# Three PSUM tiles in place of two and a remainder for the transposed q and k, and the threshold searches moved to other batches, in a top-32 attention followed by a squared-ReLU block

## The chip, the cores and the metric

The kernel runs on one core of a Trainium2 chip. The metric is the device time of one execution in microseconds (us); the median of three runs stands for a kernel. One further execution was recorded by the hardware profiler, and all rows shown come from it. The engines are TensorE (PE, with its weight loads shown apart as PEld), VectorE (DVE), ScalarE (ACT), GpSimd (POOL) and the DMA queue of SyncE (SP).

## The reference

Eight batches, eight heads, 576 positions, head size 64. Each row of scores keeps its 32 largest values, softmax is taken over these, and the result goes through two dense layers with a squared ReLU between them.

```python
scores = scale * np.matmul(q, k.transpose(0, 1, 3, 2))        # 8 x 8 x 576 x 576
kth = np.partition(scores, -32, axis=-1)[..., -32:-31]
scores = np.where(scores >= kth, scores, -1e9)
attn = np.exp(scores - scores.max(-1, keepdims=True)); attn /= attn.sum(-1, keepdims=True) + 1e-9
x = (attn @ v) with the heads of a row side by side           # 4608 x 512
out = np.maximum(x @ w_in, 0) ** 2 @ w_out                    # 512 -> 2048 -> 512
```

## The kernel before

Work on the attention is cut into *groups*: 128 query rows of the two heads of a *pair* (there are 4 pairs in a batch, 32 in all). A batch has 4 pairs by 4 full groups, and two further groups that collect the 64 rows left over of two pairs: 18 groups a batch, 144 in all.

For each pair, q and k are loaded by DMA into the tiles `rq` and `rk` (five blocks of 128 rows, the last one with 64, both heads side by side). PE transposes each block into PSUM and ACT copies the result into the tile `qk`, whose 1216 columns are q (576), the last 64 rows of k, k's 512 others, and the last 64 again. `first_pair` does this for pair 0 in its own way, `load_pair` for the 31 others. In `load_pair`, four blocks of q go into one PSUM tile `tq`, four of k into `tk`, and the two small blocks into `tx`; four ACT copies (L711 to L714) empty them. These tiles come from the pool `psum`, which has two banks of PSUM and also serves the output of the attention and of the dense layers.

For each group, `score` computes the scores on PE into three banks of PSUM, and ACT copies them to the tile `s` (L755). Then `top_k` finds the 32nd largest of each row: DVE folds the row into maxima (L905), POOL forms what is left over from the folds in integer arithmetic (L900, three instructions), and DVE takes eight maxima and strikes them out in turn (L939, L943, L934), until L946 gives the threshold `kth`. ACT makes a mask from it (L965), PE transposes scores and mask into PSUM, ACT takes the exponential (L1021), PE multiplies by v, and POOL divides by the row sums (L1096). The dense layers follow in chunks of rows: PE, ReLU on ACT (L1140), the square on POOL or ACT (L1152, L1155), PE, a copy (L1172) and a DMA to the output.

Four of the 144 groups get their threshold in another way, by `hunt`: ACT counts how many values of a row lie above a trial threshold (six rounds of two instructions at L776, each followed by a read of the accumulator), POOL moves the trial threshold by what was counted (L783, tiny instructions), and at the end one POOL multiplication (L812) and two DVE maxima (L814) read the 32nd value off the few that are left. A hunt is put into the order of groups a number of places ahead of the group that needs it. The dictionary `HUNT` names these groups as (batch, pair, block) and the number of places. A hunted group leaves out the chain of DVE instructions of `top_k`, and POOL's three. At the end the kernel looks whether every threshold is proven; if one isn't, a second, plain program runs all over again.

Nothing is ordered by hand. A planner (`Plan.schedule`) runs when the program is built: every operation has an engine, an assumed duration, and a priority in us; whenever an engine is free in the plan, the ready operation with the lowest priority value takes it. The order so found is fixed for each engine. The chip then runs each engine in this order, with semaphores for what one needs of another, so an instruction that has to wait holds up all behind it on its engine. `tg` is the due time of a group, 5.3 us (`PER`) after the one before; round j of a hunt is due at `tg + HO + HS * j`. The planner also sets short dummy matmuls where PE would be idle.

Of the kernel before, what the change touches and what calls it, by code (L numbers as in the profile page):

```python
# [13 lines left out]
P = 128  # L14
# [370 lines left out]
def bass_top_k_attn__then__act_relu_squared_kernel(  # L385
# [24 lines left out]
    def sb(name, shape, dt=FP32, n=None):  # L410
        if n is None:
            return nc.alloc_sbuf_tensor(name, shape, dt)
        return [nc.alloc_sbuf_tensor(f"{name}{i}", shape, dt) for i in range(n)]
# [31 lines left out]
    LATE = 2.3  # L445
    LAGL = 11.07
    LAGE = 2.5
    HN, HA, HP, HZ, HS, HD, HO = .3, .86, .68, 2.18, 5, 32, 22

    ident32 = sb("ident32", [P, P])  # L450
    ident_bf = sb("ident_bf", [P, P], BF16)
# [10 lines left out]
    c16 = sb("c16", [P, 2, NGRP + 8])  # L462
    c24 = sb("c24", [P, 2, NGRP + 8])
    rzall = sb("rzall", [P, NALL])
    HUNT = {(2, 2, 3): 12, (3, 2, 3): 12, (4, 2, 3): 12, (5, 2, 3): 11}
    NH = len(HUNT)
    NSTEP = 4
    GAIN = (.014, .008, .005, .003)
# [38 lines left out]
    def tile(nm):  # L507
        return Tile(pools[nm])

    def at(t):  # L510
        x = mem[t.pool.name][t.slot]
        if t.pool.name in ("hs", "hz"):
            c = 8 if t.pool.name == "hs" else 10
            return x[:, c:c + 2 * S].rearrange("p (i c) -> p i c", i=2)
        if t.pool.name in ("s", "u"):
            n_ = 2 * (S if t.pool.name == "s" else HALF + QUART)
            return x[:, t.phase:t.phase + n_].rearrange("p (i c) -> p i c", i=2)
        return x

    def bank(t, i=0):  # L520
        return ps32[:, BASE[t.pool.name] + t.slot + i, :]
# [9 lines left out]
    act, vec, gp, pe = nc.scalar, nc.vector, nc.gpsimd, nc.tensor  # L531
# [52 lines left out]
    def tr(o, i, ident, **kw):  # L584
        return pe.matmul(o, i, ident, is_transpose=True, skip_group_check=True, **kw)  # L585
# [3 lines left out]
    def build(full, weights, pl):  # L589
# [7 lines left out]
        def load_first(b, hp, rq, rq2, rk, base):  # L597

            def part(t, src, h, tb, n_):
                r0 = 128 * tb + (64 if h and src is k else 0)  # L600
                return at(t)[:, tb:tb + n_, h, :], src[b, 2 * hp + h, r0:r0 + 128 * n_, :].rearrange(
                    "(tb p) d -> p tb d", p=P)

            def rest(t, src, r0, d0):
                x = src[b, 2 * hp, r0:r0 + 64, :]
                return at(t)[0:64, 4, :, :], bass.AP(x.tensor, x.offset, [x.ap[0], [(S + d0) * D, 2], x.ap[1]])

            def start(queue, *parts):
                return lambda: [queue.dma_start(*x()) for x in parts]

            both = bass.AP(q.tensor, q[b, 2 * hp, 0:P, :].offset, [[D, P], [S * D, 2], [1, D]])
            pl.op("sp", .1, base - 82, start(nc.scalar, lambda: part(rk, k, 0, 0, 4),
                                             lambda: rest(rk, k, REST[0], REST[1] - REST[0])),
                  w=[rk], take=[rk], sem=slot_sem, ndma=2, via="act")
            pl.op("sp", 4.0, base - 81, start(nc.sync, lambda: part(rk, k, 1, 0, 4)), w=[rk], sem=lambda o: "first", ndma=1)
            pl.op("sp", 3.5, base - 80, start(nc.sync, lambda: (at(rq)[:, 0, :, :], both)), w=[rq], take=[rq],
                  sem=slot_sem, ndma=1)
            pl.op("sp", 3.5, base - 79, start(
                nc.sync, lambda: part(rq2, q, 0, 1, 3), lambda: part(rq2, q, 1, 1, 3), lambda: rest(rq2, q, 512, 0)),
                w=[rq2], take=[rq2], sem=slot_sem, ndma=3)  # L620
# [32 lines left out]
        def load_pair(b, hp, base):  # L653
            rq, rk, rv = tile("rq"), tile("rk"), tile("rv")


            def load(t, src, rest):
                def fn():
                    r = at(t)
                    res = []  # L660
                    for h in range(2):
                        r0 = 64 if h and rest != (512, 512) else 0
                        res.append(nc.sync.dma_start(r[:, 0:4, h, :], src[b, 2 * hp + h, r0:r0 + 512, :].rearrange(
                            "(tb p) d -> p tb d", p=P)))
                    x = src[b, 2 * hp, rest[0]:rest[0] + 64, :]
                    res.append(nc.sync.dma_start(r[0:64, 4, :, :], bass.AP(
                        x.tensor, x.offset, [x.ap[0], [(S + rest[1] - rest[0]) * D, 2], x.ap[1]])))
                    return res
                return fn

            def loadv():
                r = at(rv)
                res = [nc.sync.dma_start(r[:, 4 * h:4 * h + 4, :], v[b, 2 * hp + h, 64 * h:64 * h + 512, :].rearrange(
                    "(tb p) d -> p tb d", p=P)) for h in range(2)]

                for h in range(2):
                    res.append(nc.sync.dma_start(r[64 * h:64 * h + 64, 8 + h, :], v[b, 2 * hp + h, REST[h]:REST[h] + 64, :]))
                return res

            via = not full and not state["pairs"]  # L680
            state["pairs"] += 1
            if via:
                rq2 = tile("rq")
                load_first(b, hp, rq, rq2, rk, base)
            else:
                pl.op("sp", 2.3, base - 80, load(rq, q, (512, 512)), w=[rq], take=[rq], sem=slot_sem, ndma=3,
                      bw=BW * 1.9)
                pl.op("sp", 2.3, base - 79.9, load(rk, k, REST), w=[rk], take=[rk], sem=slot_sem, ndma=3, bw=BW * 1.9)
            pl.op("sp", 2.3, base - 70, loadv, w=[rv], take=[rv], sem=slot_sem, ndma=4, bw=BW * 1.9)
            qk, vb = tile("qk"), tile("vb")  # L690
            if via:
                return first_pair(rq, rq2, rk, rv, qk, vb, base)
            tq, tk, tx = Tile(psum), Tile(psum), Tile(psum)

            def t4(o, src):
                def fn():
                    for tb in range(4):
                        ins = tr(bank(o)[:, 128 * tb:128 * tb + 128], at(src)[:, tb, :, :].rearrange("p h d -> p (h d)"), ident32[:, :])
                    return ins
                return fn  # L700

            def t5():
                for i, s in enumerate((rq, rk)):
                    ins = tr(bank(tx)[:, 64 * i:64 * i + 64], at(s)[0:64, 4, :, :].rearrange("p h d -> p (h d)"), ident32[0:64, 0:64])
                return ins

            o_q = pl.op("pe", .46, base - 45, t4(tq, rq), r=[rq], w=[tq], take=[tq, qk])
            pl.op("pe", .49, base - 44.9, t4(tk, rk), r=[rk], w=[tk], take=[tk], order=[o_q])
            pl.op("pe", .22, base - 44.8, t5, r=[rq, rk], w=[tx], take=[tx], order=[o_q])

            pl.op("act", .565, base - 42.5, lambda: act.copy(at(qk)[:, 0:512], bank(tq)), r=[tq], w=[qk])  # L711
            pl.op("act", .565, base - 42.4, lambda: act.copy(at(qk)[:, 640:1152], bank(tk)), r=[tk], w=[qk])  # L712
            pl.op("act", .245, base - 42.3, lambda: act.copy(at(qk)[:, 512:640], bank(tx)[:, 0:128]), r=[tx], w=[qk])
            pl.op("act", .205, base - 42.2, lambda: act.copy(at(qk)[:, 1152:1216], bank(tx)[:, 64:128]), r=[tx], w=[qk])  # L714
            pl.op("gp", .68, base + 5, lambda: gp.tensor_copy(at(vb)[:, :, 0:D], at(rv)[:, :, :]),
                  r=[rv], w=[vb], take=[vb])
            return qk, vb
# [534 lines left out]
        def place(b, r0, n_):  # L1252

            for i, c in enumerate(CHUNKS):
                at_ = 0
                for b_, c0, m_ in c:
                    if b == b_ and c0 <= r0 and r0 + n_ <= c0 + m_:
                        return i, at_ + r0 - c0
                    at_ += m_

        for b in range(NB):
# [4 lines left out]
            for i, (hp, gi) in enumerate(seq):  # L1266
                if not full and (b, hp, gi) in HUNT:
                    plan_.insert(len(plan_) - HUNT[b, hp, gi], (hp, gi, 1))
                    plan_.append((hp, gi, 2))
                else:  # L1270
                    plan_.append((hp, gi, 0))
            for hp, gi, kind in plan_:
                tg = T0 + PER * (state["n"] + HN * state["h"])
                hps = (hp, hp if gi != Z else hp + 1)
                for x in hps:
                    if x not in pairs:
                        pairs[x] = load_pair(b, x, tg)
# [17 lines left out]
                r0, n_ = 128 * js[0], 128 * len(js) if gi != Z else 64  # L1295
                i, col = place(b, r0, n_)
                first = xts[i] is None
# [14 lines left out]
                for i, many, m_, ops in done:  # L1312
                    turned.setdefault(i, []).extend(ops)
                    left[i] -= m_ * many
                    c = CHUNKS[i]
# [210 lines left out]
```

## Time and profile before

| | |
|---|---|
| three runs | 774.7, 775.11, 775.67 us; median 775.11 us |
| profiled execution | 774.41 us, its span 772.6 us |
| busy share of the span | DVE 97%, ACT 93%, PE 92%, POOL 89% |
| granted TensorE clock, mean | 0.998 |

The page counts an instruction as busy from its start to its reported end; on ACT and DVE the next instruction often starts before that end, so that a group's "mean ns" is longer than the room which one instruction takes in the engine's row. The room is read from the starts of neighbours that follow one another without a wait. The rows of the waits say which engine stood idle, for what, how long in all, how often, and how long at most. In the rows of the stretches, the columns are the stretch, its length, the busy time of PE, PEld, DVE, ACT and POOL (with the count of instructions), the granted clock, the DMA share and the GB/s.

### The profile page before, as it was taken

To read this page: it belongs to the slowest core of one execution; us is meant where nothing else is said; L and a number is where in the kernel's file an instruction comes from. 1 tells how busy PE (TensorE), PEld (TensorE's weight loads), DVE (VectorE), ACT (ScalarE), POOL (GpSimd) and SP (SyncE) were. 2 spreads that over 40 slices of the span, in tenths; PEclk is the share of its full clock that TensorE was granted. 3 is DMA by queue.
4 is the path that set the end of the run, shared out by engine and by line. 5 is a ranking of instruction groups with operands and counts; after the bars stand their busy time and mean duration, and the time that the engine had idled before them with its cause. 6 is when DMAs were issued, how large, how long until landed. Compare 5 with 4: busy or idle time off the path is not lost.

```text
span 772.6 us, 27813 instructions
## 1 busy us (share of the span) xinstructions
PE 713.3 (92%) x10680; PEld 528.2 (68%) x10680; DVE 751.6 (97%) x3589; ACT 717.9 (93%) x1141; POOL 687.6 (89%) x720
## 2 busy tenths in 40 slices
PE   7888888999989999998999889999899999999999
PEld 3656666666666676666767657686677777767776
DVE  5999999999999999999999999899999999999996
ACT  4799989899899999999999999999999999998884
POOL 4898998889789899989999899899999998989991
PEclk9999999999999999999999999999999999999999
DMA  7657452032400134103340043301332021100101
GB/s 191 182 137 196 132 135 52 23 83 48 114 11 9 51 83 95 32 16 85 70 99 10 18 111 86 69 6 46 93 82 67 11 68 38 34 23 23 36 23 34
DMA packets 145033, 52.63 MB, mean 68 GB/s; under 512 B 137088, under 2 KB 137344, under 8 KB 144896
## 3 DMA queue, kind: packets, MB, share of 16 engines
q1 hardware_dynamic: 144224, 50.66, 26.7%
q8 instruction: 84, 1.38, 0.8%
q14 instruction: 53, 0.43, 0.2%
q10 hardware_dynamic: 672, 0.16, 0.1%
HBM read 36.70 MB, written 9.44 MB: 60 GB/s over the span
## 4 chain that ended last, share of the span: by engine, by line
ACT 58%; PE 31%; DVE 8%; issue 2%; DVEq 0%; ACTq 0%
PE ps L582 26%; ACT w L965 13%; ACT p L1021 12%; ACT s L755 12%; ACT g L1140 7%; PE ps L585 5%; ACT hz L776 4%; ACT g L1155 3%; DVE f L943 2%; DVE f L905 2%; ACT o L1172 2%; DVE c L939 2%; ACT av L1087 2%; ACT qk L711 1%; ACT qk L712 1%
## 5 line engine op out<-in xcount | busy, mean ns | idle before, releaser
L900 POOL TENSOR_TENSOR f<-u,f 128x864 int32<-128x864 int32 x138 | 236.7, 1715 | 7.6
L965 ACT ACTIVATE w<-s,kth 128x576 bf16<-128x576 f32 x278 | 220.2, 829 | 3.5 <-DVE kth L946 3.5
L943 DVE MATCH_REPLACE8 f<-c,f 128x98 f32<-128x98 f32 (+2 forms) x840 | 221.2, 270 | 0.0
L939 DVE MAX8 c<-f 128x8 f32<-128x98 f32 (+2 forms) x840 | 201.5, 272 | 0.0
L582 PE MATMUL ps<-qk 64*128 64x384 f32 (+3 forms) x1280 | 179.5, 427 | 6.9 <-DVE f L905 5.8
L900 POOL TENSOR_TENSOR u<-f,s 128x576 int32<-128x576 int32 x138 | 166.5, 1206 | 16.6 <-DVE f L905 15.9
L1021 ACT ACTIVATE p<-ps 128x1152 bf16<-128x1152 f32 x144 | 169.1, 1174 | 12.5 <-PE ps L582 11.9
L755 ACT COPY s<-ps 128x1152 f32<-128x1152 f32 x140 | 162.0, 1157 | 17.3 <-PE ps L582 16.9
L582 PEld LDWEIGHTS ps<-qk 64*128 64x128 f32 (+1 forms) x1280 | 130.5, 175 | 39.6 <-DVE f L905 11.8
L582 PE MATMUL ps<-wo,g 128*128 128x512 bf16 (+1 forms) x592 | 142.9, 375 | 2.7 <-ACT qk L714 1.2
L582 PE MATMUL ps<-xt,win 128*128 128x256 bf16 (+1 forms) x1280 | 132.5, 252 | 8.5 <-ACT g L1140 3.6
L900 POOL TENSOR_TENSOR u<-s 128x288 int32<-128x288 int32 x138 | 110.2, 799 | 29.8 <-ACT s L755 26.5
L905 DVE TENSOR_TENSOR f<-ps,f 128x288 f32<-128x288 f32 x280 | 123.7, 442 | 0.1
L946 DVE MAX8 kth<-f 128x8 f32<-128x296 f32 x280 | 120.7, 456 | 0.0
L585 PEld LDWEIGHTS ps<-ident,s 64*128 64x128 f32 x2520 | 96.8, 139 | 30.9 <-ACT w L965 15.1
L582 PEld LDWEIGHTS ps<-xt,win 128*128 128x128 bf16 x1280 | 97.2, 98 | 29.3 <-ACT g L1140 6.0
L934 DVE MAX8 f<-f 128x8 f32<-128x288 f32 x280 | 114.7, 447 | 0.0
L585 PE MATMUL ps<-ident,s 64*128 64x64 f32 x2520 | 107.0, 227 | 4.6 <-ACT w L965 4.1
L1152 POOL TENSOR_TENSOR g<-g 128x512 bf16<-128x512 bf16 x86 | 89.4, 1042 | 2.9 <-ACT g L1140 2.6
L582 PEld LDWEIGHTS ps<-wo,g 128*128 128x128 bf16 x592 | 49.6, 98 | 55.2 <-issue 5.7
L1140 ACT ACTIVATE g<-ps 128x512 bf16<-128x512 f32 x140 | 86.2, 641 | 1.0 <-PE ps L582 0.9
L582 PEld LDWEIGHTS ps<-vb,p 128*128 128x128 bf16 (+1 forms) x1600 | 54.0, 100 | 32.7 <-ACT g L1140 10.5
(104 smaller groups left out, 859.1 us busy)
## 6 DMA issues: line engine op xcount, KB each, us to landing
rv<-in_v_dram SPq DMA_DIRECT2D x64, 128.0 KB, 2.4
rk<-in_k_dram SPq DMA_DIRECT2D x63, 128.0 KB, 2.5
rq<-in_q_dram SPq DMA_DIRECT2D x62, 128.0 KB, 2.5
out_dram<-o SPq DMA_DIRECT2D x31, 256.0 KB, 2.2
g<-in_moe_w_in_dram SPq DMA_DIRECT2D x8, 512.0 KB, 4.2
g<-in_moe_w_out_dram SPq DMA_DIRECT2D x8, 512.0 KB, 4.3
out_dram<-o SPq DMA_DIRECT2D x10, 128.0 KB, 2.3
rq<-in_q_dram SPq DMA_DIRECT2D x32, 32.0 KB, 2.5
```

The lines of the kernel that those rows point to most:

```text
L582: return pe.matmul(o, l, r, start=start, stop=stop, skip_group_check=True)
L585: return pe.matmul(o, i, ident, is_transpose=True, skip_group_check=True, **kw)
L755: cp = [pl.op("act", 1.1, tg - LEAD + 1, lambda: act.copy(at(st)[:, :, 0:S], two(banks(ss)[:, FIRST_AT:], SECOND, S)), r=[ss], w=[st])]
L900: return pl.op("gp", dur, prio, lambda: gp.tensor_tensor(o().bitcast(I32), x().bitcast(I32), y().bitcast(I32), op), **kw)
L905: return dve(.36, lambda: vec.tensor_tensor(o(), two(banks(ss)[:, FIRST_AT + c:], SECOND, QUART), x(), ALU.max), r=[ss], **kw)
L934: prev[i] = [dve(.065 + HALF / 960, lambda i=i: vec.max(at(f)[:, i, A + 7:A - 1:-1], at(f)[:, i, M + QUART:E]), after=prev[i] + [low], hol ...
L939: lambda i=i, t=t, c0=c0, c1=c1: vec.max(eighth(t, i), at(f)[:, i, c0:c1]),
L943: lambda i=i, t=t, c0=c0, c1=c1: vec.match_replace(at(f)[:, i, c0:c1], eighth(t, i), at(f)[:, i, c0:c1], NEG), hold=[f])]
L946: ks.append(chain(kth, i, prev[i], .065 + (8 + HALF) / 960, lambda i=i: vec.max(eighth(kth, i), at(f)[:, i, A:M + QUART]), hold=[f]))
L965: masks[i:] = [pl.op("act", .77, tw + .8 * i, lambda i=i: act.activation(at(wt)[:, i, :], at(st)[:, i, 0:S], ACTF.Relu, bias=kth[:, i, n:n ...
L1021: return act.activation(at(pt)[:, :, :].rearrange("p c (h q) -> p h c q", h=2), bass.AP(x.tensor, x.offset, [x.ap[0], [APART, 2], [64, 9], ...
L1140: return act.activation(at(g)[:, 0:kf * nt], bank(hh)[:, 0:kf * nt], ACTF.Relu)
```

## The change

For the 31 pairs of `load_pair`, the 1216 columns of `qk` are now filled in their own order from three PSUM tiles: 384 columns (three blocks of q), 384 (the fourth block of q, the small ones of q and k, the first block of k) and 448 (three blocks of k and its small one a second time). That is eleven transposes instead of ten, and three copies instead of four. The durations assumed by the planner change with them. The four searches go to batches 1, 2, 4 and 6, each 12 places ahead (they were in 2, 3, 4 and 5, the last one 11 places ahead), and the rounds of a search are due 4 us apart instead of 5.

```diff
-    HN, HA, HP, HZ, HS, HD, HO = .3, .86, .68, 2.18, 5, 32, 22
+    HN, HA, HP, HZ, HS, HD, HO = .3, .86, .68, 2.18, 4, 32, 22
...
-    HUNT = {(2, 2, 3): 12, (3, 2, 3): 12, (4, 2, 3): 12, (5, 2, 3): 11}
+    HUNT = {(1, 2, 3): 12, (2, 2, 3): 12, (4, 2, 3): 12, (6, 2, 3): 12}
...
-            def t4(o, src):
+            def turns(o, blocks):
                 def fn():
-                    for tb in range(4):
-                        ins = tr(bank(o)[:, 128 * tb:128 * tb + 128], at(src)[:, tb, :, :].rearrange("p h d -> p (h d)"), ident32[:, :])
+                    c = 0
+                    for src, tb in blocks:
+                        n_ = 64 if tb == 4 else P
+                        ins = tr(bank(o)[:, c:c + n_], at(src)[0:n_, tb, :, :].rearrange("p h d -> p (h d)"), ident32[0:n_, 0:n_])
+                        c += n_
                     return ins
                 return fn
 
-            def t5():
-                for i, s in enumerate((rq, rk)):
-                    ins = tr(bank(tx)[:, 64 * i:64 * i + 64], at(s)[0:64, 4, :, :].rearrange("p h d -> p (h d)"), ident32[0:64, 0:64])
-                return ins
-
-            o_q = pl.op("pe", .46, base - 45, t4(tq, rq), r=[rq], w=[tq], take=[tq, qk])
-            pl.op("pe", .49, base - 44.9, t4(tk, rk), r=[rk], w=[tk], take=[tk], order=[o_q])
-            pl.op("pe", .22, base - 44.8, t5, r=[rq, rk], w=[tx], take=[tx], order=[o_q])
-
-            pl.op("act", .565, base - 42.5, lambda: act.copy(at(qk)[:, 0:512], bank(tq)), r=[tq], w=[qk])
-            pl.op("act", .565, base - 42.4, lambda: act.copy(at(qk)[:, 640:1152], bank(tk)), r=[tk], w=[qk])
-            pl.op("act", .245, base - 42.3, lambda: act.copy(at(qk)[:, 512:640], bank(tx)[:, 0:128]), r=[tx], w=[qk])
-            pl.op("act", .205, base - 42.2, lambda: act.copy(at(qk)[:, 1152:1216], bank(tx)[:, 64:128]), r=[tx], w=[qk])
+            first = None
+            for i, (o, to, blocks) in enumerate((
+                    (tq, 0, [(rq, 0), (rq, 1), (rq, 2)]), (tx, 384, [(rq, 3), (rq, 4), (rk, 4), (rk, 0)]),
+                    (tk, 768, [(rk, 1), (rk, 2), (rk, 3), (rk, 4)]))):
+                n_ = sum(64 if tb == 4 else P for _, tb in blocks)
+                x = pl.op("pe", .115 * len(blocks), base - 45 + .1 * i, turns(o, blocks), r=list({id(t): t for t, _ in blocks}.values()),
+                          w=[o], take=[o] if first else [o, qk], order=[first] if first else [])
+                first = first or x
+                pl.op("act", .14 + n_ / 1200, base - 42.5 + .1 * i, lambda o=o, to=to, n_=n_: act.copy(
+                    at(qk)[:, to:to + n_], bank(o)[:, 0:n_]), r=[o], w=[qk])
```

## The prediction

> **What bounds the kernel now.** I read the page first, then the busy time by stretches, then the waits of DVE.
>
> ```profile
> span 772.6 us, 27813 instructions
> PE 713.3 (92%) x10680; PEld 528.2 (68%) x10680; DVE 751.6 (97%) x3589; ACT 717.9 (93%) x1141; POOL 687.6 (89%) x720
> ```
>
> No engine is far from full, so the shares alone decide nothing. The stretches do more. The first cut is at 8.90 us, where DVE starts the first group, the second at 758.40, where it ends the last threshold.
>
> ```profile
> 0.00:8.90 8.90, 7.10 (x30) 3.22 (x30) 0.86 (x3) 2.94 (x6) 6.12 (x43) 1.00 0.59 132
> 8.90:758.40 749.50, 693.50 (x10484) 515.57 (x10483) 743.25 (x3560) 709.30 (x1124) 680.93 (x677) 1.00 0.28 68
> 100.00:200.00 100.00, 92.45 (x1369) 65.82 (x1365) 99.75 (x481) 89.80 (x135) 88.45 (x78) 1.00 0.29 70
> 300.00:400.00 100.00, 91.93 (x1394) 67.56 (x1395) 99.71 (x476) 99.83 (x164) 93.37 (x100) 1.00 0.26 63
> 400.00:500.00 100.00, 93.67 (x1467) 70.06 (x1462) 97.48 (x467) 99.49 (x164) 92.35 (x101) 1.00 0.26 58
> 500.00:600.00 100.00, 94.78 (x1420) 72.18 (x1419) 98.75 (x473) 98.64 (x164) 94.44 (x100) 1.00 0.25 60
> 600.00:700.00 100.00, 95.97 (x1503) 72.61 (x1500) 99.58 (x485) 92.99 (x148) 89.99 (x83) 1.00 0.14 37
> 700.00:758.40 58.40, 56.52 (x920) 42.77 (x920) 58.06 (x286) 50.37 (x77) 55.74 (x52) 1.00 0.08 22
> 758.40:772.60 14.20, 12.66 (x168) 9.42 (x167) 7.50 (x29) 5.69 (x13) 0.52 (x1) 1.00 0.14 45
> ```
>
> The third figure of busy time is DVE. Between the cuts it works 743.25 of 749.50 us, so 6.25 us is all that can be won there while its instructions stay as they are; they do, since four groups are searched before and after. The 8.90 us ahead belong to the first pair, which the change doesn't touch, and the 14.20 us behind to the last groups. The fourth figure, ACT, is the one that varies: 89.80 in 100 to 200, over 99 in 300 to 500, 92.99 in 600 to 700. The searches lie in the full part. DVE's idle time is in 400 to 600: 2.52 and 1.25 us, against 0.25 to 0.42 in 100 to 200 and 600 to 700. Who DVE waited for:
>
> ```profile
> DVE f L905 <- ACT s L755: 3.5, 5, 2.6
> DVE f L943 <- POOL f L900: 2.8, 2, 1.9
> DVE rzall L1094 <- ACT av L1087: 1.1, 3, 0.7
> ```
>
> Of the first row, 2.6 us is the wait that ends at 8.90. So between the cuts the largest item is the second row: two waits for POOL, 2.8 us. No row has DVE waiting for PE between the cuts.
>
> **The searches.** I asked for DVE's waits in each stretch from the score copy of a search (`hs` at L755) to the masks of its group: 209 to 290 for batch 2, 292 to 372 for batch 3, 390 to 480 for batch 4, 489 to 570 for batch 5. The answers in this order; batch 4 has none, and batch 5 has, beside the line shown, the row of 2.8 us above.
>
> ```profile
> DVE hk L814 <- POOL hz L812: 0.4, 1, 0.4
> DVE f L905 <- ACT s L755: 0.4, 1, 0.4
> ...
> DVE f L905 <- ACT s L755: 0.2, 1, 0.2
> ...
> DVE f L905 <- ACT s L755: 0.2, 1, 0.2
> ```
>
> So a search stood DVE 0.8, 0.2, 0 and 3.0 us. What makes the last one dear shows in the order of time; ACT, then POOL, then DVE:
>
> ```profile
> 489.25 1.12 ACT L755 COPY hs<-ps 128x1152 f32<-128x1152 f32 x1
> 492.21 1.13 ACT L755 COPY s<-ps 128x1152 f32<-128x1152 f32 x1
> 493.42 0.79 POOL L900 TENSOR_TENSOR u<-s 128x288 int32<-128x288 int32 x1 [1.84 <-ACT s L755]
> 494.18 1.25 POOL L1096 TENSOR_TENSOR x<-av,rzall 128x640 bf16<-128x640 f32 x1
> 496.68 1.72 POOL L900 TENSOR_TENSOR f<-u,f 128x864 int32<-128x864 int32 x1
> 498.43 0.09 DVE L943 MATCH_VALUE_LOAD f<-c,f 128x8 f32 x1 [1.93 <-POOL f L900]
> ...
> 524.18 1.05 POOL L1152 TENSOR_TENSOR g<-g 128x512 bf16<-128x512 bf16 x1
> 526.93 0.09 DVE L943 MATCH_VALUE_LOAD f<-c,f 128x8 f32 x1 [0.86 <-POOL f L900]
> ```
>
> The copy for the search goes ahead of the next group's copy on a full ACT; POOL stands 1.84 us for that copy, then has a division (L1096) in front of the fold that DVE needs, and DVE stands 1.93. In the second wait a square (L1152) is in front, and no instruction of a search.
>
> What a search adds to ACT is its rounds, one round for both heads being four instructions:
>
> ```profile
> 449.00 1.52 ACT hz L776 x4
> ```
>
> Six rounds at this price are 9.1 us (an upper estimate, as the first round works on fewer columns). Two searches move: 9.1 us of ACT leave batch 3 (around 300 to 380) and batch 5 (490 to 560), and come to batch 1 (between 100 and 200) and batch 6 (600 to 700). The stretch 100 to 200 has 10.2 us idle on ACT, the stretch 600 to 700 has 7.0: the first takes it, the second is 2.1 us short, with 8.0 us idle following in 700 to 758.4.
>
> Removed: 3.0 (batch 5) and 0.2 (batch 3). Added: two searches. Their cost isn't in the trace; it lies between 0 (batch 4) and 3.0 each (batch 5), and below zero there is no reason for it, as a search takes no DVE wait away where it goes. I take the mean of batches 2, 3 and 4, 0.33 each, because there too POOL had no division in front of the fold at the moment when ACT was late, and because the new places have more idle ACT than the old. Sum: -3.2 + 0.7 = -2.5 us.
>
> The spacing of 4 in place of 5 lets the last of the five later rounds be due 5 us earlier. It adds no instruction. It puts five rounds of 1.52 us into 20 us of due times, where they had 25; ACT's full stretches decide what comes of it: bounds -0.8 (all that the searches of batches 2 and 4 cost DVE now) and, for these two, the 3.0 us each of the dearest one. I take 0, the price of batch 4, whose search ran on the fullest ACT of all.
>
> **The copies.** The mean durations, and how four of the starts follow one another:
>
> ```profile
> L711 ACT COPY qk<-ps 128x512 f32<-128x512 f32 x31 | 19.8, 646 | 1.0 <-PE ps L585 1.0
> L712 ACT COPY qk<-ps 128x512 f32<-128x512 f32 x31 | 20.1, 659 | 0.8 <-PE ps L585 0.8
> L713 ACT COPY qk<-ps 128x128 f32<-128x128 f32 x31 | 10.7, 356 | 0.0
> L714 ACT COPY qk<-ps 128x64 f32<-128x64 f32 x31 | 9.5, 316 | 0.0
> ...
> 202.33 0.59 ACT L711 COPY qk<-ps 128x512 f32<-128x512 f32 x1
> 202.81 0.79 ACT L965 ACTIVATE w<-s,kth 128x576 bf16<-128x576 f32 x1
> ...
> 206.65 0.29 ACT L713 COPY qk<-ps 128x128 f32<-128x128 f32 x1
> 206.79 0.26 ACT L714 COPY qk<-ps 128x64 f32<-128x64 f32 x1
> 206.89 0.83 ACT L965 ACTIVATE w<-s,kth 128x576 bf16<-128x576 f32 x1
> ```
>
> By durations, four copies are 1977 ns; a straight line through 356 ns at 128 columns and 652 at 512 gives 554, 554 and 603 for the three, 0.27 us less a pair, 8.2 us in 31 pairs. That is the trap of this case: the durations overlap. By starts, the copies take 0.48, 0.14 and 0.10 us of ACT's row; from 128 to 512 columns it is 0.34 us more, 0.89 ns a column, and some 0.03 to 0.04 us fixed. The columns are 1216 before and after (512 + 512 + 128 + 64; 384 + 384 + 448), so one fixed part goes: about 0.04 us a pair, 1.2 us of ACT in 31 pairs, 0.16% of its busy time.
>
> The page ScalarE: Activation LUTs of the Trainium skill (section What ACT_TABLE_LOAD costs) gives an instruction without pointer operands 186 ns fixed, of which about 93 overlap with the next; by that the saving would be 93 ns a pair, 2.9 us of ACT in all. The starts above (0.10 us for the whole copy of 64 columns) leave no room for 93 ns fixed, so here the trace disagrees.
>
> Either way DVE doesn't wait for these copies in any row, and ACT's saving is spread over the run, at most 0.04 us within any group of 5.3. I cost it at 0. The cover is that the code sets these copies due some 40 us before the group (`base - 42.5`); if it were gone, a pair would gain no more than these 0.04 us.
>
> **The transposes.** One small block more a pair. Its price from two small blocks in a row on PE:
>
> ```profile
> 648.40 0.27 PE L585 MATMUL ps<-ident,rq 64*128 64x64 f32 x1
> 648.51 0.23 PE L585 MATMUL ps<-ident,rk 64*128 64x64 f32 x1
> ```
>
> 0.11 us from start to start, 3.4 us of PE in 31 pairs; the lower bound is 0, where it overlaps its neighbours. No wait of DVE leads to PE, so it lies beside DVE's work. Were that cover gone, only the pairs still to be transposed after 500 us (about 8, until 648) would meet a PE at 95% and more: 0.9 us. The PSUM pool still lends three tiles a pair; the last one is now held for a copy of 448 columns, where it was held for 128 and 64. PE's waits for that last return are few:
>
> ```profile
> PEld ps L582 <- ACT qk L714: 5.4, 9, 1.5
> ```
>
> Nine waits, 5.4 us. Each grows by the longer last copy, 0.42 against 0.24 us, so 1.6 us of PE at most, and the two other tiles come back 0.11 us earlier each. Both ends are small beside PE's idle time between the cuts (56 us), and I cost it at 0. The DMAs of q, k and v are unchanged in number and size, and no queue is reordered by hand.
>
> **Sum.** On the profiled execution: 774.41 (span 772.6 and 1.8 around it) - 2.5 = 771.9 us. The median of the runs lies 0.7 us higher, at 775.11, so the forecast is 772.6 us. A difference of 0.2% (1.6 us) is about what a measurement can tell.
>
> **The rivals.**
>
> *The searches jam where they come to (slower).* In 600 to 700 PE is at 95.97% and ACT would be 2.1 us over full; the planner, working from its own durations, puts every engine's order anew, so that a division or a square may again stand in front of DVE's fold. If the two new searches cost what batch 5 cost, it is -3.2 + 6.0 = +2.8: 777.9 us. If the closer rounds make all four cost 3.0, it is 12.0 - 4.0 = +8.0: 783.1. It decides from the point where the named waits of DVE in the four stretches sum to more than the 4.0 us of before. For it: DVE has nothing to give, any wait is lost, and the order of all 27813 instructions changes, not only that of the searches. Against it: ACT's idle time at the new places. Chance 0.37.
>
> *The waits only change place (no difference).* The second wait of batch 5 (0.86) had no search in it and may stay in some form. Then 1.9 + 0.4 go, and two searches at batch 2's price, 1.6, come: -0.7, so 774.4 us. Chance 0.14.
>
> *All of DVE's idle time goes.* ACT relieved of 8.2 us, as the mean durations would have it, is never late again, and DVE runs through: -6.25, so 768.9 us. The starts speak against it. Chance 0.03.
>
> *A search fails.* Then the second program runs, and PE's 713 us of work come nearly all again. Worked through with the reference's inputs, the four steps of the search end with 24 to 31 values above the threshold in every one of the 256 rows of each of the four groups, which is what the last step can take, also with the first threshold shifted by one part in a thousand. Chance 0.01.
>
> **How the numbers follow.** The forecast, 772.6, has 0.45. Faster by over 0.2%: 0.45 + 0.03 = 0.48. Within: 0.14. Slower: 0.37 + 0.01 = 0.38. The forecast's own range is 770.3 (half of DVE's remaining 3.7 us between the cuts goes too) to 773.5. The whole range reaches up through the first price of the slower rival to about midway between its two prices, 780.5, which leaves out some 13%, and down to 770.2, which leaves out some 4%.
>
> **What would show it.** Right: DVE's busy time between the cuts stays within 1 us of 743; its idle time there falls to about 3.7; the waits on POOL at L943 are gone; three copies with starts about 0.37, 0.37 and 0.42 us ahead of their followers; ACT's busy time rises in 100 to 200 and 600 to 700 and falls in 300 to 400 and 500 to 600; the tail behind the last threshold stays at 14.2. Wrong: new waits of DVE for POOL or for the score copy near the searches of batches 1 and 6, or a tail that is longer because PE in 600 to 758 fell behind.

## The result, and the profile after

The changed kernel takes 781.75 us (median of four runs, 781.03 to 782.17), before 775.39 (four runs). The ratio is 1.0079, 95% interval 1.0065 to 1.0092: slower by 6.4 us. The profiled execution took 781.61 us, its span is 779.8. The first line of the page and the busy times, then the stretches; the cuts are again the start of the first fold on DVE (9.54) and the end of the last threshold (764.20).

```profile
span 779.8 us, 27860 instructions
PE 720.8 (92%) x10713; PEld 533.7 (68%) x10713; DVE 754.9 (97%) x3589; ACT 719.7 (92%) x1110; POOL 687.7 (88%) x720
...
0.00:9.54 9.54, 7.75 (x30) 3.28 (x30) 0.86 (x3) 2.93 (x6) 6.46 (x46) 1.00 0.60 133
9.54:764.20 754.66, 701.12 (x10540) 521.56 (x10539) 745.56 (x3562) 710.72 (x1092) 678.58 (x672) 1.00 0.27 67
764.20:779.80 15.60, 11.96 (x144) 8.82 (x144) 8.49 (x25) 6.07 (x14) 2.69 (x3) 1.00 0.13 42
100.00:200.00 100.00, 88.25 (x1324) 65.71 (x1323) 98.40 (x469) 96.78 (x154) 91.11 (x97) 1.00 0.27 62
200.00:300.00 100.00, 94.47 (x1403) 70.99 (x1402) 96.44 (x458) 97.91 (x156) 89.77 (x96) 0.98 0.23 57
600.00:700.00 100.00, 95.62 (x1499) 72.15 (x1497) 98.55 (x473) 98.75 (x164) 92.61 (x102) 1.00 0.13 34
```

The 7.2 us of span fall into three parts: 0.6 ahead of the first fold, 5.2 between the cuts (754.66 against 749.50), 1.4 behind. The first part isn't the change's: the same place lies between 8.9 and 10.0 us in the profiles of all kernels below, whatever was edited. Between the cuts DVE is idle 9.10 us, 2.85 more than before, and busy 2.3 more. Most of its idle time lies in 200 to 300 (3.56 us) and around the other searches. DVE's waits:

```profile
DVE f L905 <- ACT s L755: 7.8, 10, 2.6
...
DVE f L943 <- POOL f L900: 0.9, 2, 0.6
```

What was forecast of the old jams came: the waits for POOL fell from 2.8 to 0.9 us. What was not: the waits for the score copy between the cuts rose from 0.9 to 5.2 us (7.8 less the 2.6 at the start). DVE's waits from the score copy of a search to the masks of its group (115 to 197 us for batch 1, then 209 to 292, 397 to 479 and 588 to 672 for 2, 4 and 6), those of 0.2 us left out:

```profile
DVE f L905 <- ACT s L755: 0.9, 1, 0.9
DVE f L943 <- POOL f L900: 0.6, 1, 0.6
...
DVE f L905 <- ACT s L755: 2.9, 3, 1.8
...
DVE f L943 <- POOL f L900: 0.3, 1, 0.3
...
DVE f L905 <- ACT s L755: 0.7, 2, 0.4
```

With the small ones the four stretches cost 1.5, 3.1, 0.7 and 0.7 us: 6.0 in all, against 4.0 before. The dearest is in the search of batch 2, which had cost 0.8 us and now costs 3.1.

```profile
213.99 0.72 ACT L776 ACTIVATE hz<-hs 128x576 f32<-128x576 f32 x1
214.67 0.70 ACT L776 ACTIVATE hz<-hs 128x576 f32<-128x576 f32 x1
215.34 1.15 ACT L1021 ACTIVATE p<-ps 128x1152 bf16<-128x1152 f32 x1
216.35 0.80 ACT L965 ACTIVATE w<-s,kth 128x576 bf16<-128x576 f32 x1
217.01 1.15 ACT L755 COPY s<-ps 128x1152 f32<-128x1152 f32 x1
...
218.19 0.46 DVE L905 TENSOR_TENSOR f<-ps,s 128x288 f32<-128x288 f32 x1 [1.84 <-ACT s L755]
```

Two instructions of a search round, an exponential and a mask stand ahead of the copy that DVE needs. The other part of the added time, DVE's busy time, is at the end:

```profile
758.51 0.44 DVE L1400 TENSOR_SCALAR fcmp<-hth 128x8 f32<-128x8 f32 x1
758.86 1.08 DVE L1402 TENSOR_SCALAR fh<-htt 128x8 f32<-128x8 f32 x1
759.98 0.17 DVE L1403 TENSOR_TENSOR fh<-fh,hth 128x8 f32<-128x8 f32 x1
760.18 0.17 DVE L1404 TENSOR_SCALAR fcmp<-fh 128x8 f32<-128x8 f32 x1
...
758.87 1.04 POOL L1152 TENSOR_TENSOR g<-g 128x512 bf16<-128x512 bf16 x1
```

Four tiny instructions of the proof that the searched thresholds hold stand in front of the last group; in before the first of them stood at 581 us and the three others behind the last threshold. One of them, eight elements a row, took 1.08 us; it starts with a square on POOL and ends with it (759.94 and 759.91). The same instruction took 0.16 us in before, with no POOL work beside it.

### The profile page after: what moved, and what is told of

The parts are those of the page before. It is cut to its first block, busy times and chain, and to the rows that moved or that the text cites. A ratio compares the mean times of both kernels' runs of the same rounds, so it can differ in the third digit from the quotient of the medians.

```text
span 779.8 us, 27860 instructions
## 1 busy us (share of the span) xinstructions
PE 720.8 (92%) x10713; PEld 533.7 (68%) x10713; DVE 754.9 (97%) x3589; ACT 719.7 (92%) x1110; POOL 687.7 (88%) x720
## 4 chain that ended last, share of the span: by engine, by line
ACT 45%; PE 34%; DVE 14%; POOL 5%; issue 2%; DVEq 0%
PE ps L582 28%; ACT s L755 10%; ACT p L1021 10%; ACT w L965 9%; PE ps L585 6%; ACT g L1140 6%; DVE f L943 4%; ACT hz L776 3%; DVE c L939 3%; DVE f L905 3%; ACT g L1155 2%; ACT qk L713 2%; POOL u L900 2%; DVE f L934 2%; DVE kth L946 2%
## 5 line engine op out<-in xcount | busy, mean ns | idle before, releaser
L965 ACT ACTIVATE w<-s,kth 128x576 bf16<-128x576 f32 x278 | 214.9, 806 | 5.9 <-DVE kth L946 5.5
L939 DVE MAX8 c<-f 128x8 f32<-128x98 f32 (+2 forms) x840 | 199.2, 273 | 0.0
L755 ACT COPY s<-ps 128x1152 f32<-128x1152 f32 x140 | 160.1, 1143 | 17.2 <-PE ps L582 16.4
L1021 ACT ACTIVATE p<-ps 128x1152 bf16<-128x1152 f32 x144 | 166.3, 1155 | 7.7 <-PE ps L582 7.4
L946 DVE MAX8 kth<-f 128x8 f32<-128x296 f32 x280 | 122.3, 458 | 0.0
```

Of the source, the lines that this page charges most:

```text
L755: cp = [pl.op("act", 1.1, tg - LEAD + 1, lambda: act.copy(at(st)[:, :, 0:S], two(banks(ss)[:, FIRST_AT:], SECOND, S)), r=[ss], w=[st])]
L939: lambda i=i, t=t, c0=c0, c1=c1: vec.max(eighth(t, i), at(f)[:, i, c0:c1]),
L946: ks.append(chain(kth, i, prev[i], .065 + (8 + HALF) / 960, lambda i=i: vec.max(eighth(kth, i), at(f)[:, i, A:M + QUART]), hold=[f]))
L965: masks[i:] = [pl.op("act", .77, tw + .8 * i, lambda i=i: act.activation(at(wt)[:, i, :], at(st)[:, i, 0:S], ACTF.Relu, bias=kth[:, i, n:n ...
L1021: return act.activation(at(pt)[:, :, :].rearrange("p c (h q) -> p h c q", h=2), bass.AP(x.tensor, x.offset, [x.ap[0], [APART, 2], [64, 9], ...
```

## The experiments

Three questions: which of the three edits costs; whether it is the work that they change or the order that the planner makes of it; and, once the tiles had been found to cost in the old order too, which part of them. The expectations call the answers theories or rivals: 1, where the searches stand; 2, any new order; 3, the work of the tiles, with 3a the eleventh block, 3b the changes between blocks of 128 and 64 rows (here: of *height*), 3c the copies.

**Each edit alone, and an order left as it was.** `e1_tiles` is the new transposes and copies with `HUNT` and `HS` of before; `e2_searches` and `e3_spacing` are one line each:

```diff
-    HUNT = {(2, 2, 3): 12, (3, 2, 3): 12, (4, 2, 3): 12, (5, 2, 3): 11}
+    HUNT = {(1, 2, 3): 12, (2, 2, 3): 12, (4, 2, 3): 12, (6, 2, 3): 12}     # e2_searches
-    HN, HA, HP, HZ, HS, HD, HO = .3, .86, .68, 2.18, 5, 32, 22
+    HN, HA, HP, HZ, HS, HD, HO = .3, .86, .68, 2.18, 4, 32, 22              # e3_spacing
-            o_q = pl.op("pe", .46, base - 45, t4(tq, rq), ...
+            o_q = pl.op("pe", .47, base - 45, t4(tq, rq), ...                # n1_order
```

> The three tiles alone, with the searches and their spacing as before. Theory 1 (the loss is made by where the searches stand): about 775, within 2 us of before, and DVE's waits for the score copy between the first group and the last threshold stay near 0.9 us. Rival 2 (any new order of the instructions costs, since the planner's constants fit the old order): 778 to 783, with DVE's waits for the score copy risen although no search has moved. Rival 3 (the eleventh transpose and the longer last copy cost by themselves): 778 to 780, with the waits at the qk copies on PE risen by 3 us or more.

> The searches alone go to batches 1, 2, 4 and 6; tiles and spacing as before. Theory 1: about 781, nearly the whole loss, with DVE's waits for the score copy in 200 to 300 at about 3 us as in the changed kernel. Rival 2: anywhere from 777 to 783, with the waits at other places than in the changed kernel. Rival 3: about 772 to 775, the gain that was forecast.

> The spacing of 4 alone; tiles and batches as before. Theory 1: 775 to 777, as the four searches keep their places. Rival 2: 777 to 783, as this too makes a new order. Rival 3: 775.

> The kernel before, with one duration assumed by the planner for the transposes of q raised from 0.46 to 0.47 us: the same instructions in number and kind, only the planner's order can differ. Theory 1 and rival 3: 774 to 776, no work was changed. Rival 2: 777 to 783, if the order differs at many places.

Measured: tiles 779.83 us (ratio 1.0057, 1.0040 to 1.0074), searches 778.00 (1.0027, 1.0013 to 1.0041), spacing 779.62 (1.0053, 1.0036 to 1.0070), each against 775.13. `n1_order`: 775.53 (1.0002, 0.9992 to 1.0011); its order turned out to be that of before on DVE, ACT and POOL, and to differ on PE mainly in the place of two matmuls of the dense layers, so it only shows how well a kernel of the same order repeats. Theory 1 (the searches' places make the loss) falls: each edit alone costs, the three add to 12 us where together they cost 6.4, and the spacing costs nearly as much as the tiles although no instruction is added or moved to another batch. The searches are where DVE waits, all the same. In `e1_tiles`, with the searches in their old batches 2 to 5, the four stretches (209 to 290, 300 to 385, 395 to 479, 494 to 574) have, waits under 0.4 us left out:

```profile
DVE f L943 <- POOL f L900: 0.4, 1, 0.4
...
DVE f L943 <- POOL f L900: 2.9, 3, 1.6
...
DVE f L905 <- ACT s L755: 1.7, 2, 1.2
DVE f L943 <- POOL f L900: 0.6, 2, 0.4
...
DVE f L943 <- POOL f L900: 2.4, 2, 1.9
```

All told that is 0.7, 3.1, 2.3 and 2.6 us, 8.7 against the 4.0 of before; in `e3_spacing` it is 7.3.

**The same work in another order.** Only durations that the planner is told are edited; the instructions of before stay, in number and shape:

```diff
-            pl.op("act", .565, base - 42.5, lambda: act.copy(at(qk)[:, 0:512], ...
+            pl.op("act", .555, base - 42.5, lambda: act.copy(at(qk)[:, 0:512], ...   # z_act1
-            o_q = pl.op("pe", .46, base - 45, t4(tq, rq), ...
+            o_q = pl.op("pe", .50, base - 45, t4(tq, rq), ...                         # z_both (with .53 and .235 for the
                                                                                      # other two, .545, .545, .238 for copies), z_pe50 (alone)
```

> The kernel before, with the planner told that the first qk copy takes 0.555 us where it was told 0.565. No instruction is added, dropped or resized; the planner's order changes at most places. Rival 2: 777 to 782, like each of the three edits alone (778.0 to 779.8), with new waits of DVE for POOL or for the score copy. Rivals 1 and 3: 774 to 776.

> The kernel before, with the planner told of 0.50, 0.53 and 0.235 us for the transposes (0.46, 0.49, 0.22 before) and 0.545, 0.545 and 0.238 for three of the copies (0.565, 0.565, 0.245 before). The same instructions in another order. Rival 2: 777 to 782. Rivals 1 and 3: 774 to 776.

> The kernel before with the planner told of 0.50 us in place of 0.46 for the transposes of q. About half as many places of the order differ as in the other reorderings, and the plan's length is that of before, 771.3 us. Theory 2 with the plan's length: 775 to 777. If any other order costs: 777 to 782.

> The kernel before with other durations told to the planner for its transposes and copies; the plan's length is that of before, 771.3 us, and the order differs on DVE and ACT at most places. Theory 2 with the plan's length: 775 to 777. If before is one lucky order and the plan's length tells nothing: 779 to 782, like the two other reorderings of before.

Measured: `z_act1` 782.10 us (ratio 1.0083, 1.0056 to 1.0110), `z_both` 781.91 (1.0077, 1.0056 to 1.0098), `b_other` 778.18 (1.0029, 1.0016 to 1.0043), `z_pe50` 776.74 (1.0021, 1.0006 to 1.0036). Telling the planner 0.01 us less for one copy costs as much as the whole change. DVE's waits in `z_act1`, then in `z_both`:

```profile
DVE f L905 <- ACT s L755: 6.4, 8, 2.6
DVE f L943 <- POOL f L900: 4.0, 6, 1.2
...
DVE f L943 <- POOL f L900: 6.1, 7, 1.9
DVE f L905 <- ACT s L755: 3.9, 7, 2.6
```

The same two rows as in before (3.5 and 2.8 us), grown by an instruction standing in front of another. In `z_both` DVE is besides busy for 3.3 us more between the first fold and the last threshold (746.57 against 743.25): the proof's four instructions stand in the middle of the kernel there, beside POOL's integer work, and three of them are stretched, to 1.36, 0.76 and 1.14 us; the first of them, and what ran on POOL:

```profile
580.85 1.36 DVE L1400 TENSOR_SCALAR fcmp<-hth 128x8 f32<-128x8 f32 x1
580.47 1.71 POOL L900 TENSOR_TENSOR f<-u,f 128x864 int32<-128x864 int32 x1
```

The two smaller costs go with the clock. `b_other` took 775.64 to 776.46 us in its three runs with a granted clock of 0.998 and 778.05 to 779.52 in the seven with 0.991 or 0.993; `z_pe50` took 775.5 to 776.37 in five runs with 1.0 and 777.11 to 780.33 in five with 0.996 or 0.998. At the higher clock neither is clearly slower than before, whose median beside them was 775.76; whether the order brings the lower clock, or chance, isn't shown.

The order of before is a good one among many: of 150 plans that the kernel's planner makes of before when its seven durations for transposes and copies are drawn within 6%, none is shorter than its 771.3 us by the planner's own sum, and the middle one is 775.7 long (these are plans; they were not run). The chip follows that sum roughly: 771.3 gave 775.1, 776.7 and 778.2, and 775.5 and 776.5 gave 781.9 and 782.1. The changed kernel's plan is 774.1 long.

**The changed work in other orders.** `a_short` and `a_early` are the changed kernel with `.115` and `.14 + n_ / 1200` told otherwise:

> The changed kernel with other durations told to the planner for the new transposes and copies (0.1095 us a block, 0.132 us and 1/1242 us a column): the same instructions as in the changed kernel in another order, whose plan is as long as that of before, 771.3 us by the planner's own sum (774.1 in the changed kernel). Theory 2 (the order decides, and the plan's length tells much of it): 775 to 778. Theory 1 and 3 (the places of the searches or the work of the tiles cost 5 us and more in any order): 780 to 783.

> The changed kernel, again with other durations told to the planner (0.112, 0.1302, 1/1224): in this plan DVE's last instruction ends at 766.2 us (766.7 in before, 770.3 in the changed kernel), while the plan as a whole is 774.0 long, as in the changed kernel. Theory 2 with DVE's end deciding: 775 to 778. Theory 2 with the whole length deciding: 780 to 783. Theories 1 and 3: 780 to 783.

Measured: 779.78 us (ratio 1.0060, 1.0041 to 1.0079) and 782.99 (1.0107, 1.0090 to 1.0123). The short plan brings 2.0 us, not the 4 to 7 that it should if the order were all; DVE's early end in the plan brings nothing. So with plans of equal length the changed work is still 1.6 to 4.7 us behind that of before, and some of the loss seems to lie in the work; the next experiment shows it without a change of order.

**The new tiles inside the old order.** The planner is given the operations of before; only what they emit is new, and a copy of the last column fills the place of the fourth copy. DVE and POOL keep their order exactly, ACT and PE theirs by operation:

```diff
-            o_q = pl.op("pe", .46, base - 45, t4(tq, rq), r=[rq], w=[tq], take=[tq, qk])
-            pl.op("pe", .49, base - 44.9, t4(tk, rk), r=[rk], w=[tk], take=[tk], order=[o_q])
-            pl.op("pe", .22, base - 44.8, t5, r=[rq, rk], w=[tx], take=[tx], order=[o_q])
+            o_q = pl.op("pe", .46, base - 45, turns(tq, [(rq, 0), (rq, 1), (rq, 2)]), r=[rq], w=[tq], take=[tq, qk])
+            pl.op("pe", .49, base - 44.9, turns(tk, [(rk, 1), (rk, 2), (rk, 3), (rk, 4)]), r=[rk], w=[tk], take=[tk], order=[o_q])
+            pl.op("pe", .22, base - 44.8, turns(tx, [(rq, 3), (rq, 4), (rk, 4), (rk, 0)]), r=[rq, rk], w=[tx], take=[tx], order=[o_q])
```

> The new transposes and copies (three tiles of 384, 384 and 448 columns, the small block of k twice) inside the old plan: the planner is given the operations and durations of before, so that every engine keeps its old order. The copy of the first 383 columns of the third tile is followed by one of its last column, so that ACT keeps four copies. Rival 3 (the work of the tiles costs): 778 to 780, like the tiles in their own order, which took 779.8. Rival 2 (the new order costs, not the work): 774 to 776.5, within 1.5 us of before, the four copies together taking about 1.2 us of ACT's row a pair as before.

Measured: 780.65 us (ratio 1.0073, 1.0052 to 1.0093). Rival 2 alone falls as well: 5.5 us with no order changed on DVE. The same pair on PE in before, then here; "x4" are four blocks in a row, and the last line of each on PE is the scores; then the clock in the stretch that follows (0.57), and ACT and DVE there:

```profile
382.35 0.66 PE L585 MATMUL ps<-ident,rk 128*128 128x128 f32 x4 [0.92 <-ACT g L1140]
382.93 0.27 PE L585 MATMUL ps<-ident,rq 64*128 64x64 f32 x1
382.94 0.59 PE L582 MATMUL ps<-qk 64*128 64x384 f32 x1
...
384.31 0.75 PE L585 MATMUL ps<-ident,rk 128*128 128x128 f32 x4 [1.03 <-ACT g L1140]
384.99 0.53 PE L585 MATMUL ps<-ident,rq 128*128 128x128 f32 x2
385.36 0.48 PE L585 MATMUL ps<-ident,rk 64*128 64x64 f32 x2
385.77 1.81 PE L582 MATMUL ps<-qk 64*128 64x192 f32 x7
...
386.00:390.00 4.00, 3.67 (x47) 3.15 (x47) 3.02 (x17) 3.13 (x5) 3.92 (x4) 0.57 0.58 130
387.64 1.12 ACT L755 COPY s<-ps 128x1152 f32<-128x1152 f32 x1 [0.55 <-PE ps L582]
388.79 0.46 DVE L905 TENSOR_TENSOR f<-ps,s 128x288 f32<-128x288 f32 x1 [0.97 <-ACT s L755]
```

From the first transpose of k to the scores it is 0.59 us in before, 1.46 us here. About half of the difference is that eight blocks stand there in place of four, among them a block of q that before had turned earlier; the rest is changes of height. In before the two small blocks, 64 rows high like the scores, run beside them (0.01 us apart). Here they stand between blocks of 128 rows, and each change of height costs: the records have, as medians, 0.11 us from start to start between blocks of one height, 0.20 from 128 rows to 64, 0.15 from 64 to 128 (in `x_switch` below 0.26 and 0.20). The page TensorEngine Tiling (Array Packing) of the Trainium skill (section Key Properties) states that changing the tiling mode drains TensorE; the starts agree, with 0.09 and 0.04 us. Here the scores come late besides with the clock granted at 0.57 in the four microseconds after, and ACT waits 0.55 us for them and DVE 0.97 for their copy. In this profile 2.0 of the 5.5 us arise between 375 and 400 us, around that one place; how much of that is the halved clock's and not the transposes' isn't shown.

**Which part of the tiles.** Order, copies and searches of before for the first two; the third is the kernel just shown with the third tile's blocks in another sequence.

```diff
-                for i, s in enumerate((rq, rk)):
+                for i, s in enumerate((rq, rk, rk)):                                      # x_dup
+                for c, s, tb, n_ in ((0, rq, 4, 64), (128, rk, 0, 128), (64, rk, 4, 64)):  # x_switch
-            ... turns(tx, [(rq, 3), (rq, 4), (rk, 4), (rk, 0)]) ...
+            ... turns(tx, [(rq, 4, 128), (rk, 4, 192), (rq, 3, 0), (rk, 0, 256)]) ...      # u_grouped (third figure: column)
```

> The kernel before with one small transpose more a pair: the small block of k is turned a second time into columns of the third tile that nobody reads. Order, copies and searches are those of before. If the eleventh block by itself costs (theory 3a): 777 to 780. If only the changes between 128-row and 64-row blocks or the copies cost (3b, 3c): 775 to 776.5, for 3.4 us of PE spread over 31 pairs.

> The kernel before with one transpose of 128 rows put between the two small ones, into columns that nobody reads, so that each pair has two more changes between 64-row and 128-row blocks and about 0.25 us more of PE. Order, copies and searches are those of before. Theory 3b (the changes of rows make PE late, and with it the scores): 777.5 to 781, with DVE's waits for the score copy up from 3.5 to 6 us or more. Theory 3c (the larger third copy costs): 775 to 776.5.

> The new transposes and copies inside the old plan as before (780.65), with the blocks of the third tile turned small ones first, so that they follow on the small one at the end of the second tile: up to two changes of rows less a pair. Theory 3b: 777 to 779.5. Theory 3c or 3a: 780 to 781.5.

| in the old order | changes of height at the transposes | PE for the transposes, us | time, us | ratio (95%) |
|---|---|---|---|---|
| before | 90 | 47.0 | 775.1 | |
| x_dup | 90 | 49.1 | 775.76 | 1.0011 (1.0001 to 1.0020) |
| u_grouped | 130 | 54.4 | 777.02 | 1.0021 (1.0012 to 1.0031) |
| x_switch | 152 | 57.7 | 778.10 | 1.0042 (1.0029 to 1.0054) |
| t_same_order | 180 | 59.7 | 780.65 | 1.0073 (1.0052 to 1.0093) |

The second column counts, in the profiled execution, neighbours on PE of different height of which one is a transpose of q or k; the third sums the time from the start of each such transpose to PE's next start, at most 0.3 us each. Each ratio is against runs of before on the same chip (774.83 for the three in the middle, 775.14 for the last). The eleventh block by itself costs 0.8 us. The changes of height go with the rest. `u_grouped` and `t_same_order` have the same blocks, copies and order of operations and differ only in the sequence of four blocks: 50 changes, 3.6 us by the medians. `x_switch` has the copies of before, so they aren't needed for the loss, but its eleventh block has 128 rows; it is 3.2 us slower, `u_grouped` by its own ratio 1.6. Less 0.8 for the block, that is 0.02 to 0.05 us a change counted from before, and 0.07 between the last two rows: no fixed price. DVE's waits for the score copy in `x_dup`, `u_grouped`, `x_switch` and `t_same_order` show the way it takes, if not all of the time (before has 3.5, and 4.0 in `n1_order` with the same order):

```profile
DVE f L905 <- ACT s L755: 3.7, 6, 2.6
...
DVE f L905 <- ACT s L755: 4.4, 8, 2.6
...
DVE f L905 <- ACT s L755: 4.7, 10, 2.6
...
DVE f L905 <- ACT s L755: 7.7, 14, 2.6
```

**The proof's instructions, and the changed kernel with its blocks grouped.**

```diff
-            fcmp[:, 2 * G:2 * G + 2 * NH], flat(hth[:, :, :]), 0.0, None, ALU.is_le), after=checks)
+            fcmp[:, 2 * G:2 * G + 2 * NH], flat(hth[:, :, :]), 0.0, None, ALU.is_le), after=checks + kths)   # v_verdict, and
                                                                                       # the same for the next one (htt)
-  (tx, 384, [(rq, 3), (rq, 4), (rk, 4), (rk, 0)]), (tk, 768, [(rk, 1), (rk, 2), (rk, 3), (rk, 4)])
+  (tx, 384, [(rq, 3, 0), (rk, 0, 256), (rq, 4, 128), (rk, 4, 192)]), (tk, 768, [(rk, 4, 384), (rk, 1, 0), ...])  # w_grouped, with v_verdict
```

> The changed kernel, with the two first small DVE instructions of the proof that the searches' thresholds hold made to wait for all thresholds, so that they can't stand ahead of the last groups' work on DVE; the order of the other engines is the same. In the changed kernel these four instructions took from 758.5 to 760.3 us ahead of the last threshold. If they lie on the path: 1.0 to 1.8 us below the changed kernel's 781.75, 780.0 to 780.7. If the last thresholds are paced by something else: 781.5 to 782.

> The changed kernel with the proof's instructions kept behind the last thresholds (779.87 by itself) and the small blocks of the second and third tile turned one after the other, every engine's order otherwise as in the changed kernel. Theory 3b: 777 to 779. Otherwise 779.5 to 780.5.

> The changed kernel with the proof's instructions behind the last thresholds, again, beside the next one: 779.5 to 780.5.

> The same with the small blocks grouped, which takes the changes of rows around the transposes from 174 to 124. Theory 3b, at the 0.05 to 0.06 us a change that the four kernels in the old order show: 2.5 to 3 us below the one beside it, 777 to 778. If the order's own waits hide it: within 1 us of the one beside it.

Measured: `v_verdict` 779.87 us (779.58 to 780.73; ratio 1.0055, 1.0037 to 1.0074), 1.9 below the changed kernel, whose runs begin at 781.03; the two weren't run side by side. In `a_short` these instructions stand behind the last threshold too, so its 2.0 us may be the same gain and not the shorter plan's. `w_grouped` 779.29 with a wide interval (1.0044 to 1.0098; three of its nine runs, at 781.04 to 787.9 us, had the clock granted at 0.993 and less), which settled nothing; side by side, `v_verdict_again` 780.03 (779.48 to 780.65; 1.0056, 1.0044 to 1.0068) and `w_grouped_again` 778.48 (778.08 to 778.91; 1.0037, 1.0025 to 1.0049). So 50 changes of height less bring 1.6 us in the changed kernel's order, where 50 less brought 3.6 in the old one and 2.5 to 3 were expected. With both mended the change still stands at 778.5. None of these beats before.

## Why the prediction was wrong

It forecast 772.6 with 0.45 and a range to 780.5; 781.75 lies above it. The sign belongs to the rival with 0.37, whose two prices (777.9 and 783.1) enclose the time and whose own sign was met: DVE's waits in the four stretches sum to 6.0 us, above 4.0. Its reason was half right. The waits do gather at the searches, but not because these moved: with the searches left where they were, the new tiles bring 8.7 us there and the new spacing 7.3.

*What bounds the kernel*: right. DVE has the same 3589 instructions. Of the 5.2 us lost between the cuts 2.85 are its waits and 2.3 its busy time, which was to stay within 1 us of 743 and is 745.56, most of that at the proof's instructions.

*The searches, -3.2 + 0.7*: the first step that failed. ACT's work moved as forecast (89.80 to 96.78 us in 100 to 200, 92.99 to 98.75 in 600 to 700, 99.83 to 93.30 in 300 to 400), and the waits for POOL fell (2.8 to 0.9), but the four stretches, which were to cost 1.5 us, cost 6.0: the two that stayed, taken over at 0.8 and 0, cost 3.1 and 0.7. What a search costs in one order doesn't carry to the next, and this term can't be read apart from the order. The searches moved alone cost 2.9 us, within the 1.0 to 7.0 us of the reorderings without any change of work; whether the new places are better or worse in themselves stays open. The prediction's second rival, that the waits only change place, came nearer, except that they also grew.

*The copies, 0*: right in size. The new copies start 0.36 and 0.42 us ahead of their followers, as worked out, while by mean duration they seem to have saved 0.40 us a pair (503, 503 and 570 ns against 1977 for the four):

```profile
L713 ACT COPY qk<-ps 128x384 f32<-128x384 f32 x62 | 30.4, 503 | 0.9 <-PE ps L585 0.8
L713 ACT COPY qk<-ps 128x448 f32<-128x448 f32 x31 | 17.7, 570 | 0.2 <-PE ps L585 0.2
...
253.79 0.75 ACT L713 COPY qk<-ps 128x448 f32<-128x448 f32 x1
254.21 1.01 ACT L776 ACTIVATE hz<-hs,hk 128x583 f32<-128x583 f32 x1
...
296.24 0.54 ACT L713 COPY qk<-ps 128x384 f32<-128x384 f32 x1
296.60 0.86 ACT L965 ACTIVATE w<-s,kth 128x576 bf16<-128x576 f32 x1
```

*The transposes, 0.11 us a pair, 3.4 us of PE, hidden*: the second step that failed, in its size and in its cover. PE's row for them grew from 47.0 to 57.7 us in the changed kernel (174 changes of height), 0.34 us a pair. The price was taken from two small blocks in a row and left out what lies between a small and a large one. And "No wait of DVE leads to PE, so it lies beside DVE's work" read only the last link: DVE waits for ACT's score copy, and that copy for PE, as the place at 387.64 us shows. The tiles in the old order cost 5.5 us, in their own order 4.7, where the prediction had 0 and, without the cover, 0.9.

*The order, 0*: the third step that failed. The slower rival did say that the planner "puts every engine's order anew", but no term of the sum priced that. Four reorderings with no change of work cost 1.0, 2.4, 6.8 and 7.0 us (the first two perhaps by the clock), so a forecast of -2.5 us rested on terms smaller than this one. The planner's own sum could have been asked before any run: 774.1 us for the changed kernel against 771.3.

*The tail*: taken as unchanged at 14.2; it is 15.6, and why stays open. Ahead of it, the proof's instructions, which neither the sum nor a rival had, cost 1.9 us.

*The range*: half of the remaining 3.7 us leads to 770.7, not to the 770.3 given; nothing rests on it.

The parts don't add up one by one: tiles, searches and spacing alone come to 12 us, and each makes an order of its own. What is shown is that the new tiles cost 5.5 us in the old order, 3.6 of it by the sequence of heights alone, that the placing of the proof costs about 1.9 us in the new one, and that a change of order alone can cost 7 us. How the 6.4 us divide between these stays open.

## What to carry to other kernels

In a kernel whose order a planner fixes and whose constants were chosen on that order, price a new order by itself: reorder the old work without changing it, and see how far the time moves, before you put a small saving on the scale. Ask the planner for the length of the new plan, which costs no run, though it tells the time only roughly. Follow a wait of the bounding engine back through every link, since a transpose on PE reached DVE by way of a copy on ACT. Keep blocks of one height together on PE, next to other work of that height.

## What the runs showed of the hardware

On PE, from start to start, fp32 transposes of one height take 0.11 us, a change from 128 rows to 64 takes 0.20 to 0.26 and from 64 to 128 0.15 to 0.20 (medians in `t_same_order` and `x_switch`), while 64-row transposes run beside 64-row matmuls 0.01 us apart.

A DVE instruction of eight elements a row took 1.08 us beside a square on POOL that ended with it, and 0.16 us without; in `z_both` another took 1.36 us and ended at 582.21, an integer instruction on POOL at 582.18. The page SBUF — State Buffer of the Trainium skill (section SBUF: two separate sides) has GpSimd and DVE, in some forms of its instructions, share a port pair that one of them holds for a whole instruction; the two ends, 759.94 and 759.91 us, agree, though no run here takes the POOL instruction away.

The clock granted to TensorE halved (0.50) for 3.4 us at a time in most of the profiles: at 21 us in before, at 386 in `t_same_order` (0.57 on average in 386 to 390), at 272 in the changed kernel. The places aren't the kernel's alone: one execution of the same program has them at 168 and 635 (`v_verdict`), another at 272 (`v_verdict_again`). What sets it off isn't shown.
